# Pooled attention in a fused attention and two-MLP kernel: split float32r operands replaced by plain float32 on halves of the TensorE array

## The chip, the cores and the metric

One Trainium2 chip, one of its cores. The metric is the device time of the whole program in microseconds. The kernel before takes 675.1 us (median of three runs, 675.06 to 675.31). The engines are named as in the profile: PE is TensorE (PEld its weight loads), DVE is VectorE, ACT is ScalarE, POOL is GpSimd, SP is SyncE, whose queue issues most DMAs.

## The reference

All inputs are float32: q, k and v of 2 batches x 8 heads x 1152 positions x 64, then two MLPs on the 1152 x 512 result.

```python
q_pool = q.reshape(B, H, S // 2, 2, D).mean(axis=3)        # 576 rows a head
scores = scale * np.matmul(q_pool, k.transpose(0, 1, 3, 2)) # 576 x 1152
scores = scores - np.max(scores, axis=-1, keepdims=True)
attn = np.exp(scores)
attn = attn / (np.sum(attn, axis=-1, keepdims=True) + 1e-09)
x = np.matmul(attn, v)                                      # then heads side by side: 1152 x 512
h = x @ w_in
g = s * np.maximum(h, 0) ** 2 + b
y = g @ w_out                                               # w_in 512 x 2048
out = ((y @ w_a) * (y @ w_b)) @ w_out2                      # w_a, w_b 512 x 1536
```

## The kernel before, in words

The 16 heads are worked through as eight pairs, `n` = 0 to 7. In a pair the 2 x 576 pooled rows of q make nine blocks of 128 rows (`ORDER`): four of the first head, a middle one with 64 rows of each head, four of the second. Block `i` of pair `n` has the number `g = 9 * n + i`.

Products are made in float32r, each operand as a high part and a low part (what the high part misses). A key tile `kc` holds the high parts of k in 64 of 128 columns and the low parts in the others, so that turned (transposed by a product with the identity, `k_tr`) both stand below each other on the 128 rows of the array. A block of scores is the turned k against `qh`, then against `ql`, in three pieces of 384 columns: two into one tile of two banks (`s_mm01`), the third into a bank of its own (`s_mm2`). The middle block takes twice as many, with `qm_h` and `qm_l`.

Then, for each block: two maxima on DVE and their combination (`s_max01`, `s_max2`, `s_comb`); exp with a running sum on ACT in pieces of 384 and 768 columns (`s_exp2`, `s_exp01`); the sum and its reciprocal on DVE; the multiplication of `e` by it on POOL (`s_norm`, L491). Nine turns on PE (L515) put `e` into PSUM in groups of four, four and one, where the third group's bank also takes three riding turns of k or pooled q for the next pair. ACT copies the turned block out as its high part (`p_h`, L529), DVE subtracts that for the low part (`p_l`, L535). P by v (`pv_mm`, L551) runs over nine chunks of 128 keys, high and low, for each head in one segment of 256 and one of 320 rows; v stands beside its low part in the 128 columns of the stationary operand. Results are copied out by ACT (L563), moved between partition halves by DMA on SP's queue (`pv_add`, six a pair), added on POOL and split into `xa_h` and `xa_l` (`x_split`, L94 and L97), the first MLP's input. POOL also pools q (L338) and splits k and v (L94, L97).

There are three `e` buffers, two two-bank tiles for the main scores, and four banks (`banks`) that last scores, turns and P by v take in turn (`bank`, `bank_read`).

The order of all engines' work is written out by hand: `SCHED` is one period, in which each word is a step and a block or chunk, and each prime puts the step one pair later. `steps()` unrolls it over the eight pairs, a few steps are then moved by name (`put`), and each engine works off its own instructions strictly in that order. At the last pair the order also takes in the first products of the first MLP (`MM`, with `Fa`, `Fd`, `Fp` on ACT, DVE and POOL) and weight conversions (`CV`). The MLPs that follow (L681, L1005) aren't touched by the change.

Of the kernel before, what the change touches and what calls it, by code (L numbers as in the profile page):

```python
# [27 lines left out]
A.0 PP.8' X2.1 Lb.7' EVh.8' P2.4' R.0 Fp.0''''''''''''''' hc.8' M01.2 Tb.8' Lc.8' P2.5' S2.2 hb.8' Lb.8' P2.6' Ta.8'
X01.1 M2.2 A.1 ha.8' N.0 C.2 P2.7' R.1 P2.8' PVc.2' Tb.0 PVd.2' S01.3 hb.0 La.8' X2.2 Lb.0
CV.8''''''''''''''''''''''''''''''''''''''''''''''''''''''''''' N.1 S2.3 PP.1 M2.3 Ta.0 PP.0 X01.2 Tc.1 ha.0 M01.3  # L30
EVh.1 La.0 hc.1 Tc.0 EVh.0 C.3 KS.0, hc.0 MM.0' EVl.1 Lc.1 X2.3 S01.4 S2.4 A.2 Ta.1 Lc.0 X01.3 Tb.1 R.2 ha.1 P3.0'
M01.4 P3.1' M2.4 A.3 La.1 hb.1 Lb.1 CV.0, P3.2' S01.5 N.2 P3.3' Tb.2 R.3 C.4 hb.2 Ta.2 XS.0' P3.4' P3.5' ha.2 P3.6'
N.3 M01.5 X2.4 Lb.2 P3.7' P3.8' MM.1''''''''''''''''''''''''''''''''''''''''''''''' La.2 X01.4 CV.6' CV.7' CV.2 S2.5
PP.2 Tc.2 PVc.3' CV.1, Tb.3 EVh.2 M2.5 S01.6 P0.0 PVd.3' P0.1 hc.2 Lc.2 P0.2 S2.6 P0.3 C.5 hb.3 Lb.3 A.4 PP.3 X2.5
X01.5 Fd.0'''''' QP.0, Tc.3 Ta.3 M01.6 EVh.3 P0.4 R.4 M2.6 hc.3 P0.5 ha.3 VS.1 Fa.0'' CV.4 S01.7 A.5 N.4 C.6 Lc.3 S2.7
R.5 X01.6 P0.6 P0.7 P0.8 La.3 X2.6 Ta.4 M01.7 A.6 Tb.4 M2.7 PVc.0 R.6 ha.4 N.5 XS.1' CV.5 PVd.0 hb.4 Tc.4 C.7 PP.4
S01.8 La.4 X2.7 Ta.5 Lb.4 hc.4 Tc.5 PP.5
""".split()

@with_exitstack  # L40
def kernel(
# [212 lines left out]

# [4 lines left out]

# [911 lines left out]
```

## Time and profile before

| | us |
|---|---|
| median of three runs | 675.1 |
| the profiled execution | 675.21 |
| its span, first to last instruction | 673.4 |
| PE busy (98% of the span) | 662.3 |
| DVE busy (76%) | 512.4 |
| ACT busy (59%) | 394.9 |
| POOL busy (53%) | 354.1 |
| mean granted TensorE clock, share of full speed | 0.999 |

The busy times are sums over the whole span, and the span has two parts: the attention up to about 260 us, in which all four engines are in use, and the MLPs after it, which are mostly PE's. Shares of the whole say little about either; the rows below are from stretches of the attention.

### The profile page before, as it was taken

How to read it: one execution, taken by the hardware profiler on the slowest of the kernel's cores; microseconds unless marked ns; L12 is line 12 of the kernel's file. 1: busy time of each engine (PE TensorE's matmuls, PEld its weight loads, DVE VectorE, ACT ScalarE, POOL GpSimd, SP SyncE). 2: the span in 40 equal slices, each digit the busy share in tenths (PEclk: the TensorE clock that was granted, in tenths of full speed). 3: DMA queues.
4: the chain of work that ended last, by engine and by line, in shares of the span. 5: the costliest groups of instructions: out<-in, count | busy, mean ns of one | idle time of the engine just before them, and what ended most of it. 6: DMA issues, size and time to landing. Idle time of an engine off the chain costs nothing.

```text
span 673.4 us, 12031 instructions
## 1 busy us (share of the span) xinstructions
PE 662.3 (98%) x4446; PEld 635.8 (94%) x4446; DVE 512.4 (76%) x1007; ACT 394.9 (59%) x869; POOL 354.1 (53%) x316
## 2 busy tenths in 40 slices
PE   7999999999999999999999999999999999999997
PEld 6899999999999989999999999999999999988885
DVE  6999999999999995683554654888988787886431
ACT  6999999999999984464442242335343434434321
POOL 5779897978889693775454553400424542340000
PEclk9999999999999999999999999999999999999999
DMA  7122231413221023331322311420132323233004
GB/s 235 46 81 70 65 89 51 120 39 96 57 85 50 14 74 92 100 124 62 108 82 63 125 63 63 151 100 1 63 126 68 121 70 120 70 112 133 0 1 140
DMA packets 29275, 56.04 MB, mean 83 GB/s; under 512 B 2336, under 2 KB 6048, under 8 KB 29216
## 3 DMA queue, kind: packets, MB, share of 16 engines
q1 hardware_dynamic: 29136, 55.14, 26.0%
q8 instruction: 35, 0.57, 0.3%
q14 instruction: 24, 0.20, 0.1%
q10 hardware_dynamic: 80, 0.13, 0.1%
HBM read 49.81 MB, written 2.36 MB: 77 GB/s over the span
## 4 chain that ended last, share of the span: by engine, by line
PE 91%; DVE 3%; POOL 1%; DMA 1%; ACT 1%; issue 1%; SPq 0%; POOLq 0%; ACTq 0%; DVEq 0%
PE ps L681 29%; PE pp L681 17%; PE pv L551 11%; PE pp L1005 11%; PE s L423 8%; PE t L515 8%; PE s L430 4%; PE t L363 2%; PE t L383 1%; DMA xs<-tmp 1%; DMA qm<-in_q_dram 1%; DVE e L947 1%; DVE wl L165 0%; POOL e L491 0%; DVE f L143 0%
## 5 line engine op out<-in xcount | busy, mean ns | idle before, releaser
L491 POOL TENSOR_SCALAR e<-e,sm 128x1152 f32<-128x1152 f32 (+1 forms) x73 | 88.9, 1222 | 29.2 <-DVE sm L484 16.0
L1020 POOL TENSOR_TENSOR ab<-ab,at 128x576 f32<-128x576 f32 x24 | 35.0, 1478 | 91.1 <-ACT ab L1015 87.2
L515 PE MATMUL t<-identr,er 128*128 128x128 f32 x648 | 76.9, 245 | 2.9 <-POOL e L491 1.6
L515 PEld LDWEIGHTS t<-identr,er 128*128 128x128 f32 x648 | 65.4, 140 | 11.5 <-POOL e L491 2.4
L819 POOL TENSOR_SCALAR r<-r,sb_s,sb_b 128x384 f32<-128x384 f32 (+1 forms) x46 | 38.5, 848 | 61.0 <-DVE r L816 61.0
L535 DVE TENSOR_TENSOR p3l<-t,p3h 128x512 fp32r<-128x512 f32 (+1 forms) x120 | 64.6, 552 | 5.9 <-ACT p3h L529 4.3
L452 DVE TENSOR_REDUCE sm<-s 128x1 f32<-128x768 f32 x72 | 68.2, 947 | 0.1
L472 ACT ACTIVATE e<-s,sm 128x768 f32<-128x768 f32 x72 | 67.1, 932 | 0.5 <-DVE sm L460 0.4
L529 ACT CAST p3h<-t 128x512 fp32r<-128x512 f32 (+1 forms) x120 | 55.5, 506 | 10.3 <-PE t L515 9.5
L811 ACT ACTIVATE qpl<-ps 128x384 f32<-128x384 f32 (+1 forms) x46 | 21.7, 503 | 67.7 <-PE ps L681 62.7
L816 DVE SCALAR_TENSOR_TENSOR r<-ps,qpl 128x384 f32<-128x384 f32 (+1 forms) x46 | 25.1, 570 | 37.7 <-ACT qpl L811 37.6
L535 DVE TENSOR_TENSOR p2l<-t,p2h 128x512 fp32r<-128x512 f32 (+1 forms) x96 | 51.3, 549 | 1.6 <-ACT p2h L529 1.1
L141 ACT ACTIVATE f<-raw 128x1024 f32<-128x1024 f32 x34 | 38.6, 1135 | 17.7 <-issue 11.1
L529 ACT CAST p2h<-t 128x512 fp32r<-128x512 f32 (+1 forms) x96 | 46.7, 519 | 3.1 <-PE t L515 1.2
L681 PE MATMUL ps<-xa_h,wh 128*128 128x384 f32 (+1 forms) x200 | 45.2, 329 | 0.6 <-DVE r L816 0.6
L551 PE MATMUL pv<-p3h,v 128*128 128x320 f32 x144 | 45.7, 328 | 0.0
L464 ACT ACTIVATE e<-s,sm 128x384 f32<-128x384 f32 x72 | 43.7, 607 | 2.2 <-DVE sm L460 1.4
L681 PE MATMUL ps<-xa_l,wh 128*128 128x384 f32 (+1 forms) x200 | 45.0, 328 | 0.0
L681 PE MATMUL ps<-xa_h,wl 128*128 128x384 f32 (+1 forms) x200 | 45.0, 328 | 0.0
L165 POOL TENSOR_TENSOR wl<-f,wh 128x1024 fp32r<-128x1024 f32 x16 | 40.5, 2528 | 7.1 <-ACT wh L197 5.9
L681 PE MATMUL ps<-gh,wl 128*128 128x384 f32 x192 | 43.7, 336 | 0.0
L681 PE MATMUL ps<-gh,wh 128*128 128x384 f32 x192 | 43.7, 336 | 0.0
(142 smaller groups left out, 2036.6 us busy)
## 6 DMA issues: line engine op xcount, KB each, us to landing
raw<-in_moe_w_out_dram SPq DMA_DIRECT2D x14, 1024.0 KB, 4.9
raw<-in_moe_w_in_dram SPq DMA_DIRECT2D x8, 1024.0 KB, 5.5
raw<-in_moe_w_a_dram SPq DMA_DIRECT2D x6, 1024.0 KB, 5.0
raw<-in_moe_w_b_dram SPq DMA_DIRECT2D x6, 1024.0 KB, 5.0
vn<-in_v_dram SPq DMA_DIRECT2D x8, 576.0 KB, 3.9
...
```

The source lines that it names most:

```text
L165: eng.tensor_tensor(out=l, in0=f, in1=h.bitcast(F32), op=ALU.subtract)
L423: nc.tensor.matmul(ps[:, c, 0:384], w, x[:, c * 384:(c + 1) * 384], start=(z == 0), stop=(z == len(pr) - 1))
L452: nc.vector.reduce_max(small(g)[:, 0:1], SPS[g, 0][:, :, 0:384], axis=AX.XY)
L464: ins = nc.scalar.activation(out=e_tile(g)[:, 768:1152], in_=SPS.pop((g, 1))[:, 0:384], func=AF.Exp, bias=m[:, 2:3], accum_out=m[:, 3:4])
L472: ins = nc.scalar.activation(out=e_tile(g)[:, 0:768].rearrange("p (a c) -> p a c", a=2), in_=SPS.pop((g, 0))[:, :, 0:384], func=AF.Exp, bi ...
L491: E_DONE[g, c.start] = nc.gpsimd.tensor_scalar(out=e[:, c], in0=e[:, c], scalar1=m[:, 6:7], scalar2=1.0, op0=ALU.mult, op1=ALU.mult)
L515: t = nc.tensor.transpose(ps[:, i * 128:(i + 1) * 128].bitcast(F32R), er_at[g % 3][:, (c0 + i) * 128:(c0 + i + 1) * 128], identr)
L529: nc.scalar.copy(out=p_dst(g)[0][:, c0:c0 + n], in_=p_src(g, z))
L535: nc.vector.tensor_tensor(out=l, in0=p_src(g, z), in1=h.bitcast(F32), op=ALU.subtract)
L551: nc.tensor.matmul(ps[:, 0:N], V[n, hd][:, c].rearrange("p a d -> p (a d)"), p, start=(t == 0), stop=(t == 2 * NC - 1))
L681: nc.tensor.matmul(ps, a, c[:, o:o + n], start=(first and z == 0), stop=(last and z == 2), skip_group_check=more)
L1005: nc.tensor.matmul(ps, a[x], w2_at[kf][c], start=(kf == 0 and y == 0), stop=(kf == KF2 - 1 and y == 2))
```

## The change

The high and low parts of q, k, v and the turned blocks go. All products of the attention are plain float32.

- **Scores.** k is turned straight from the loaded tile, two chunks of 64 columns at a time, so even chunks stand on the array's upper 64 rows and odd ones on the lower (`X`, 640 columns). A main score is two 512-column products, one on each half of the rows, each into a bank of its own (`s_mm`); the ninth chunk's 128 columns follow on one half, upper or lower by the block's number (`s_mmx`). It stands in `X` twice; for that `load_k` loads it a second time. The middle block's products are split by output rows too, into quarters.
- **Turns.** `turn` makes two products, one for each half of 64 rows, with a 64-column identity, into two banks, one for each half (`ps_t`). Eight chunks of a block make a group (`p_tr`); ACT copies one bank out (`H`), DVE the other (`D`). The ninth chunks of two or three blocks come together with the turns of k or pooled q for the next pair in four further groups (`turns`, steps `U`, `UH`, `UD`).
- **P by v.** Two products of 288 columns for each chunk and head, one for each half of the array's columns, into the two partition halves of one bank (`pv_mm`). Four DMAs a pair put the results in place, with nothing to add.
- **Banks.** Four for main scores as before, two for the turns, two (`banks`) for last scores and P by v.
- **Buffers and loads.** Seven `e` buffers instead of three, two for k, and loads of k, v and q are issued up to three pairs ahead; the first loads of q go to ACT's queue.
- **Order.** A new `SCHED`, with no steps moved by name. `MM.0` of the first MLP is issued after all attention steps of the last pair.

The diff, cut to its core:

```diff
+D.5' X.7' T.6' M.0 MX.0 CV.5'' D.6' H.6' C.0 P0.3' A.7' P0.4' X.0 R.7' P0.5' U.2' UD.2' MM.0'''' S.1 UH.2' N.7' CV.2'
+P0.6' M.1 T.7' XX.0 H.7' SX.1 D.7' MX.1 S.2 C.1 T.8' A.0 R.0 XX.1 D.8' P0.7' H.8' P0.8' SX.2 X.1 M.2 MX.2 A.1 C.2 U.3'
+PVc.0' UH.3' XX.2 X.2 UD.3' S.3 M.3 SX.3 N.0 SX.4 MX.3 R.1 C.3 T.0 H.0 XX.3 S.4 D.0 M.4 MX.4 N.1 X.3 P1.0' P1.1' P1.2'
+CV.6'''' A.2 Fp.0''''''''''''''' A.3 CV.4' XS.0'' C.4 T.1
+CV.8''''''''''''''''''''''''''''''''''''''''''''''''''''''''''' R.2 R.3 D.1 S.5 XX.4 M.5 SX.5 MX.5 H.1 C.5 U.0 UD.0
+P1.3' X.4 N.3 P1.4' S.6 UH.0 N.2 X.5 T.2 S.8 XX.5 CV.1 SX.6 D.2 H.2 A.4 CV.7''''' M.6 T.3 P1.5' MX.6 P1.6' R.4 A.5 N.4
+C.6 CV.0, D.3 H.3 Fd.0''''''' P1.7' XX.6 QP.1, R.5 P1.8' X.6 M.8 PVd.0' SX.8 T.4 S.7 MX.8 PVc.1' SX.7 A.6 PVd.1' N.5
+H.4 C.8 XX.8 D.4 R.6 U.1 N.6 P0.0 M.7 X.8 QP.0,, UD.1 MM.1''''''''''''''''''''''''''''''''''''''''''''''' P0.1 A.8
+P0.2 MX.7 Fa.0'''' R.8 UH.1 T.5 C.7 S.0, XX.7 H.5 SX.0, N.8
...
     ps_s01 = s01.enter_context(tc.tile_pool(name="ps_s01", bufs=2, space=PSUM))
-    banks = [right(att, f"ps_{i}", 1, space=PSUM) for i in range(4)]
+    ps_t = [right(att, f"ps_t{i}", 1, space=PSUM) for i in range(2)]
+    banks = [right(att, f"ps_{i}", 1, space=PSUM) for i in range(2)]
+    NE = 7
+    ex_p = right(att, "ex", 1)
+    e_at += [ex_p.tile([128, S], F32, tag=f"e{i}", name=f"e{i}") for i in range(3, NE)]
+    pt = right(att, "pt", 1).tile([128, 2, NC, SP], F32, tag="pt", name="pt")
...
-    kc_p = right(att_in, "kc", 1)
+    k_p = right(att_in, "kn", 2)
+    free, held = list(range(2)), {}
...
+            KN[n] = k_p.tile([128, 2, NC + 1, D], F32, tag="kn", name="kn")
         o = slice(max(part - 1, 0), 2 if part != 1 else 1)
-        nc.sync.dma_start(out=KN[n][:, o], in_=k[b, h + o.start:h + o.stop].rearrange("h (p c) d -> p h c d", p=128))
+        src = k[b, h + o.start:h + o.stop].rearrange("h (p c) d -> p h c d", p=128)
+        nc.sync.dma_start(out=KN[n][:, o, 0:NC], in_=src)
+        nc.sync.dma_start(out=KN[n][:, o, NC], in_=src[:, :, NC - 1])
...
+    def q_step(n, hd):
+        q_pool(n, hd)
+            q_pool(n, 2)
+            load_q(n + 1)
+    def turn(ps, z, src):
+        for o, t in zip(HALF, ps):
+            nc.tensor.transpose(t[:, z * 64:z * 64 + 64], src(o), ident[o, o])
...
+        def mm(ps, w, r, c):
+            o = HALF[r]
+            if hd < 2:
+                nc.tensor.matmul(ps[:, 0:w], Q[n, hd][o, j * 128:(j + 1) * 128], X[n, hd][o, c], start=True, stop=True)
+            else:
+                for a in range(2):
+                    nc.tensor.matmul(ps[HALF[a], 0:w], Q[n, 2][o, a], X[n, a][o, c], start=True, stop=True, skip_group_check=True)
+    def s_mm(g):
+        SPS[g] = ps = ps_s01.tile([128, 2, 512], F32, tag="s01", name="s01")
+        for r in range(2):
+            s_parts(g)(ps[:, r], 512, r, slice(0, 512))
+    def s_mmx(g):
+        XPS[g] = ps = bank(("x", g), 2)
+        s_parts(g)(ps, 128, g % 2, slice(512, 640))
...
+        out = e_at[g % NE][:, 0:1024].rearrange("p (a c) -> p a c", a=2)
+        nc.scalar.activation(out=out, in_=SPS.pop(g), func=AF.Exp, bias=m[:, 2:3], accum_out=m[:, 4:5])
...
+        nc.scalar.activation(out=e_at[g % NE][:, 1024:S], in_=XPS.pop(g)[:, 0:128], func=AF.Exp, bias=m[:, 2:3], accum_out=m[:, 3:4])
+        bank_read(("x", g))
...
+        m, e = SM.pop(g), e_at[g % NE]
+        nc.gpsimd.tensor_scalar(out=e, in0=e, scalar1=m[:, 6:7], scalar2=1.0, op0=ALU.mult, op1=ALU.mult)
+    def t_tiles(key):
+        PS[key] = [p.tile([128, 512], F32, tag="t", name="t") for p in ps_t]
+        return PS[key]
+    def p_turn(ps, g, z, pos):
+        turn(ps, z, lambda o: e_at[g % NE][o, pos * 128:(pos + 1) * 128])
+    def p_tr(g):
+        ps = t_tiles(g)
+        for pos in range(8):
+            p_turn(ps, g, pos, pos)
+    def p_evac(g, k):
+        hd, j = ORDER[g % 9]
+        if hd < 2:
+            c = p_col(j) + 64 * k
+            out = pt[:, hd, 0:8, c:c + 64]
+        else:
+            out = pt[:, k, 0:8, 256:256 + NX]
+        copy(k, out, slots(PS[g], k, 0, 8))
+    TURN = [(0, 1), (2, 3, 4), (5, 6), (7, 8)]
+    def turns(n, u):
+        at = TURN[u] if n >= 0 else ()
+        if not at and n + 1 >= NP:
+            return
+        ps = t_tiles((n, u))
+        for z, i in enumerate(at):
+            p_turn(ps, 9 * n + i, z, 8)
+        if n + 1 < NP:
+            z, hd = len(at), u // 2
+            if u % 2:
+                src = qp_all.ap()
+                for j in range(4):
+                    turn(ps, z + j, lambda o: src[o, 4 * hd + j].rearrange("p a d -> p (a d)"))
+                if hd:
+                    turn(ps, z + 4, lambda o: src[o, 8].rearrange("p a d -> p (a d)"))
+                    Q[n + 1, 2] = q_p.tile([128, 2, 64], F32, tag="qt", name="qt")
+                Q[n + 1, hd] = q_p.tile([128, 512], F32, tag=f"q{hd}", name="q")
+            else:
+                for m in range(5):
+                    turn(ps, z + m, lambda o: KN[n + 1][o, hd, 2 * m:2 * m + 2].rearrange("p a d -> p (a d)"))
+                X[n + 1, hd] = x_p.tile([128, 640], F32, tag=f"x{hd}", name="x")
+                if hd:
+                    load_k(n + 3)
+    def turns_last(n, u, k):
+        if n < 0:
+            return
+        ps, hd = PS[n, u], u // 2
+        c = p_col(ORDER[TURN[u][0]][1])
+        copy(k, by_half(pt[:, hd, 8, c:c + 256], 2, k), slots(ps, k, 0, 2))
+        if u == 1:
+            copy(k, pt[:, k, 8, 256:256 + NX], ps[k][:, 128:192])
+    def turns_ride(n, u, k):
+        if n + 1 >= NP:
+            return
+        ps, z, hd = PS[n, u], len(TURN[u]) if n >= 0 else 0, u // 2
+        if u % 2:
+            copy(k, by_half(Q[n + 1, hd], 4, k), slots(ps, k, z, 4), qscale)
+            if hd:
+                copy(k, Q[n + 1, 2][:, k], ps[k][:, (z + 4) * 64:(z + 5) * 64], qscale)
+        else:
+            copy(k, by_half(X[n + 1, hd], 5, k), slots(ps, k, z, 5))
+    def pv_mm(n, hd, pos):
+        if pos == 0:
+            PV[n, hd] = bank(("pv", n, hd), 4 if (n, hd) == (NP - 1, 1) else 1)
+        ps = PV[n, hd]
+        for a in range(2):
+            nc.tensor.matmul(
+                ps[HALF[a], 0:HC], VN[n][:, hd, CHUNK[pos]], pt[:, hd, pos, a * HC:(a + 1) * HC],
+                start=(pos == 0), stop=(pos == NC - 1), skip_group_check=True,
             )
+        if hd and pos == NC - 1:
+            load_v(n + 2)
...
+        TMP[n, hd] = xs_p.tile([128, HC], F32, tag=f"t{hd}", name="tmp")
+        nc.scalar.copy(out=TMP[n, hd], in_=ps[:, 0:HC])
+        bank_read(("pv", n, hd))
+        if hd == 0:
+            XS[n] = xs_p.tile([128, SP], F32, tag="xs", name="xs")
+        for a in range(2):
+            nc.sync.dma_start(out=XS[n][HALF[hd], a * HC:(a + 1) * HC], in_=TMP[n, hd][HALF[a]])
+    def x_split(n, _):
+        o = slice(0, 128 if n < NP - 1 else 64)
+        split(*(t[o] for t in xa_at(n)), XS[n][o], nc.gpsimd, nc.gpsimd)
...
-        load_q(0, 1)
+        load_q(0, 1, nc.scalar)
-        load_q(0, 2)
+        load_q(0, 2, nc.scalar)
-        nc.vector.tensor_copy(out=identr, in_=ident)
-        for t in (qm_h, qm_l):
-            nc.vector.memset(t.bitcast(F32), 0.0)
-        warm = bank(("warm",), 1)
+        t_warm = t_tiles("warm")[0]
         for i in range(N_WARM):
-            nc.tensor.transpose(warm[:, 0:128], ident, ident)
-        bank_read(("warm",))
-        KC[0, 0] = kc_p.tile([128, NC, 2, D], F32R, tag="kc", name="kc")
-        thirds = [(KC[0, 0][:, c:c + 3], KN[0][:, 0, c:c + 3]) for c in range(0, NC, 3)]
-        for t, x in thirds:
-            nc.scalar.copy(out=t[:, :, 0], in_=x)
...
+            nc.tensor.transpose(t_warm[:, 0:128], ident, ident)
         q_pool(0, 0, nc.vector)
-        third_l(1)
-        third_l(2)
-        for t in "PP.2 PP.5 PP.3 PP.4 EVh.2 EVh.5 EVh.3 EVl.5".split():
+        early = "U.0 UH.0 UD.0 U.1 UH.1 UD.1".split()
+        for t in early:
             step(t, -1)
+        q_pool(0, 1)
+        q_pool(0, 2)
         load_q(1)
         load_k(1)
         unit_load()
-        order = list(steps())
-        order.remove(("XS.1", NP - 2))
-        order.insert(order.index(("N.6", NP - 1)) + 1, ("XS.1", NP - 2))
-        def put(t, n, behind):
-            if (t, n) in order:
-                order.remove((t, n))
-            order.insert(order.index(behind) + 1, (t, n))
-        put("EVh.4", -1, ("S01.0", 0))
-        put("PP.6", -1, ("S2.0", 0))
-        put("EVl.6", -1, ("C.1", 0))
-        put("X2.0", 0, ("X01.0", 0))
-        end = 1 + max(i for i, (t, n) in enumerate(order) if t.split(".")[0] in ("S01", "S2", "VS"))
+        load_v(1)
+        order = [(t, n) for t, n in steps() if n >= 0 or t not in early]
+        end = 1 + max(i for i, (t, n) in enumerate(order) if t.split(".")[0] in ("S", "SX"))
```

## Rows read from the trace of the kernel before

**Rows 1.** The page, part 4: the chain that ended last, by engine

```profile
PE 91%; DVE 3%; POOL 1%; DMA 1%; ACT 1%; issue 1%; SPq 0%; POOLq 0%; ACTq 0%; DVEq 0%
```

**Rows 2.** Busy by stage: length, PE, PEld, DVE, ACT, POOL, clock, DMA, GB/s

```profile
51.34:82.13 30.79, 30.75 (x244) 29.59 (x242) 29.35 (x80) 28.91 (x78) 26.27 (x26) 1.00 0.28 74
...
205.38:236.31 30.93, 30.91 (x241) 29.47 (x240) 30.55 (x81) 28.75 (x78) 24.62 (x25) 1.00 0.13 34
```

**Rows 3.** Timeline of PE, 110.1 to 128.3 us: start, length, instruction, count

```profile
110.14 0.80 PE L515 MATMUL t<-identr,er 128*128 128x128 f32 x8
110.78 0.38 PE L551 MATMUL pv<-p3h,v 128*128 128x320 f32 x1
...
119.60 0.51 PE L423 MATMUL s<-x,ql 128*128 128x384 f32 x2
119.95 0.33 PE L430 MATMUL s<-x,qh 128*128 128x384 f32 x1
...
120.41 0.28 PE L551 MATMUL pv<-p2l,v 128*128 128x256 f32 x1
120.53 0.28 PE L551 MATMUL pv<-p2h,v 128*128 128x256 f32 x1
...
128.10 0.31 PE L551 MATMUL pv<-p3h,v 128*128 128x320 f32 x1
128.25 0.30 PE L551 MATMUL pv<-p3l,v 128*128 128x320 f32 x1
```

**Rows 4.** Timeline of PE, warm-up: the second turn on, and the last two

```profile
1.62 1.06 PE L698 MATMUL warm<-ident 128*128 128x128 f32 x4
...
4.82 0.63 PE L698 MATMUL warm<-ident 128*128 128x128 f32 x2
```

**Rows 5.** Groups by form, stage 112.91 to 143.63: count, busy us, mean ns, idle before

```profile
L452 DVE TENSOR_REDUCE sm<-s 128x1 f32<-128x768 f32 x10 | 9.5, 948 | 0.0
L472 ACT ACTIVATE e<-s,sm 128x768 f32<-128x768 f32 x9 | 8.4, 935 | 0.0
...
L535 DVE TENSOR_TENSOR p3l<-t,p3h 128x512 fp32r<-128x512 f32 x10 | 6.7, 686 | 0.4 <-ACT p3h L529 0.2
L529 ACT CAST p3h<-t 128x512 fp32r<-128x512 f32 x10 | 5.9, 612 | 1.4 <-PE t L515 1.3
...
L464 ACT ACTIVATE e<-s,sm 128x384 f32<-128x384 f32 x9 | 5.5, 610 | 0.1
...
L455 DVE TENSOR_REDUCE sm<-s 128x1 f32<-128x384 f32 x9 | 5.0, 551 | 0.5 <-PE s L430 0.4
...
L97 POOL TENSOR_TENSOR kc<-kn,kc 128x576 fp32r<-128x576 f32 x2 | 2.9, 1430 | 0.2
...
L472 ACT ACTIVATION_READ_ACCUMULATOR e<-s,sm 128x1 f32 x9 | 2.1, 234 | 0.0
...
L480 DVE TENSOR_SCALAR sm<-sm 128x1 f32<-128x1 f32 x9 | 1.9, 208 | 0.0
L484 DVE RECIPROCAL sm<-sm 128x1 f32<-128x1 f32 x10 | 1.6, 156 | 0.0
...
L460 DVE TENSOR_REDUCE sm<-sm 128x1 f32<-128x2 f32 x10 | 1.5, 149 | 0.0
L529 ACT CAST p3h<-t 128x128 fp32r<-128x128 f32 x5 | 1.5, 297 | 0.0
...
L94 POOL TENSOR_SCALAR kc<-kn 128x576 fp32r<-128x576 f32 x2 | 1.4, 683 | 0.7 <-PE t L515 0.7
...
L400 ACT ACTIVATE qh<-t 128x384 fp32r<-128x384 f32 x2 | 1.1, 551 | 0.0
...
L563 ACT COPY tmp<-pv 128x320 f32<-128x320 f32 x2 | 0.9, 457 | 0.0
...
L400 ACT ACTIVATE qh<-t 128x128 fp32r<-128x128 f32 x2 | 0.6, 308 | 0.0
```

**Rows 6.** Line L1128: count, shortest, median and longest ns, first and last start

```profile
L1128 DVE COPY ab<-pp x4: 691/692/692, 657.5 to 661.5; 128x512 f32<-128x512 f32 x4
```

More of the change, by code (lines that the diff above doesn't have):

```diff
@@ L29 @@
[L29 to L33, printed above, removed]
@@ L296, in bank_read, with load_q @@
             free.append(held.pop(key)[0])
-    QN, QM, KN, VN = {}, {}, {}, {}
-    Q_READ, Q_DONE, E_READ = {}, {}, {}
-    SYNC = mybir.DependencyClass.Sync
-    def after(ins, earlier, why):
-        tc.add_manual_dep(ins.ins, earlier.ins.name, mybir.DependencyInfo(SYNC, why), reason="one room under two names")
-    KC, X, Q, V, E, RS, SPS = {}, {}, {}, {}, {}, {}, {}
+    QN, QM, KN, VN, X, Q, QT = {}, {}, {}, {}, {}, {}, {}
+    HALF = [slice(0, 64), slice(64, 128)]
     def bh(n):
         return n // HP, 2 * (n % HP)
-    def load_q(n, part=0):
+    def load_q(n, part=0, queue=nc.sync):
+        if n >= NP:
+            return
         b, h = bh(n)
@@ L504 @@
-    PTC = ((0, 4), (4, 4), (8, 1))
-    def t_bank(g, z):
-        if (g, z) not in TP:
-            TP[g, z] = bank(("t", g, z), 2 * (g >= 0) + (rides(g) if z == 2 else 0))
-        return TP[g, z]
-    def p_tr(g, z):
-        ps = t_bank(g, z)
-        c0, n = PTC[z]
-        for i in range(n):
-            t = nc.tensor.transpose(ps[:, i * 128:(i + 1) * 128].bitcast(F32R), er_at[g % 3][:, (c0 + i) * 128:(c0 + i + 1) * 128], identr)
-            if i == 0:
-                after(t, E_DONE[g, 512 if g == 0 and z else 0], mybir.DependencyReason.DATA)
-        E_READ.setdefault(g, []).append(t)
@@ L538 @@
-    TP = {}
-    PV = {}
-    XS = {}
-    def pv_mm(n, hd, big_seg, lo, hi):
-        key = (n, hd, big_seg)
-        N = 256 + NX if big_seg else 256
-        if lo == 0:
-            PV[key] = bank(("pv", key), 2 if n == NP - 1 else 1)
-        ps = PV[key]
-        for t in range(lo, hi):
-            c, x = divmod(t, 2)
-            p = p3[x][:, c, hd] if big_seg else p2[x][:, c]
-            nc.tensor.matmul(ps[:, 0:N], V[n, hd][:, c].rearrange("p a d -> p (a d)"), p, start=(t == 0), stop=(t == 2 * NC - 1))
@@ L608, in rides @@
-    def rides(g):
-        ahead, reads, _ = RIDES[g % 9]
-        return reads if g // 9 + ahead < NP else 0
-    def ride(n, i):
-        g = 9 * n + i
-        if rides(g):
-            pend[n, i] = RIDES[i][2](n + RIDES[i][0], t_bank(g, 2)[:, 128:512])
-    def evac(n, i, z):
-        if (n, i) in pend and pend[n, i][z]:
-            pend[n, i][z]()
-            bank_read(("t", 9 * n + i, 2))
-    def then_load(f, load):
-        def run(n, hd):
-            f(n, hd)
-            if hd == 1 and n + 1 < NP:
-                load(n + 1)
-        return run
+        m, e = SM.pop(g), e_at[g % NE]
@@ new lines, in xa_at, with pv_copy @@
+    def xa_at(n):
+        b, hp = divmod(n, HP)
+        return [x[:, hp, b * SP:(b + 1) * SP] for x in (xa_h, xa_l)]
+    def pv_copy(n, hd):
+        ps = PV[n, hd]
+        if (n, hd) == (NP - 1, 1):
+            h, _ = xa_at(n)
+            for a in range(2):
+                nc.scalar.copy(out=h[HALF[1], a * HC:(a + 1) * HC], in_=ps[HALF[a], 0:HC])
+                bank_read(("pv", n, hd))
+            return
+        TMP[n, hd] = xs_p.tile([128, HC], F32, tag=f"t{hd}", name="tmp")
+        nc.scalar.copy(out=TMP[n, hd], in_=ps[:, 0:HC])
+        bank_read(("pv", n, hd))
```

308 lines of the change are left out of this document (71 added, 237 removed).

## The prediction

> **What bounds the kernel now.** I read the chain that ended last first: 91% of the span is on PE [rows 1], so only time taken off PE, or a wait put in front of it, moves the end. Next I cut the attention into its repeating stages, one for each pair of heads, by the POOL instruction that writes xa_l. Six such stages follow one another from 51.34 to 236.31 us, 185.0 us together, 30.8 us each, at full granted clock [rows 2]. In each PE is busy for all but 0.04 us, DVE for 29.4, ACT for 28.9, POOL for 26.3 of the first, so PE sets the pace and DVE and ACT are only 5 to 6% behind it: a cheaper PE would soon meet them. The MLPs are untouched and PE-bound, so the sum is eight stages plus what happens at the two ends of the attention.
>
> What a PE instruction costs is the step from one start to the next, not its recorded length, which has a tail. The timeline gives 0.175 us for a 384-column score product (two in 119.60 to 119.95), 0.12 for a 256-column and 0.15 for a 320-column P by v product, 0.08 for a turn (eight from 110.14 to 110.78) [rows 3]. A stage has 60 score products (nine blocks with six, the middle one with twelve), 36 of each P by v kind and 108 turns (81 of e, 18 of k, 9 of q): 10.5 + 4.3 + 5.4 + 8.6 = 28.8 us. The 2.0 us that are left lie where the 15 groups of turns of the order meet products, 0.13 us a group; I use that as the price of a change of mode.
>
> **The change on PE.** Its products are plain float32, and the only plain float32 work in the trace is the 18 warm-up turns. Between the second, at 1.62, and the seventeenth, at 4.82, are fifteen steps, 0.213 us each [rows 4]. 128 columns at 2.4 GHz, the granted level, take 0.053 us: so plain float32 streams its columns four times, with nothing between, and the weight load hides behind it. Then, if the two halves of the array work at the same time:
> - Scores: 512 columns x 4 / 2.4 GHz = 0.853 us for a block's main part, 0.213 for its last 128 columns. Nine blocks: 9.6 us (10.5 now). The middle block runs as four quarters and costs the same.
> - P by v: 18 chunks of two 288-column products side by side, 0.48 each: 8.6 us (9.7 now).
> - Turns: 81 of e, 10 of k, 9 of q, each two 64-column products side by side, 0.107: 10.7 us (8.6 now). This part gets dearer. Its bounds: 0.107, if the loads of both halves are hidden as in the warm-up, and 0.16, if the two loads follow each other at the 0.08 of today's turns [rows 3]. I take 0.107, since the warm-up is the nearest row, float32 like the new turns.
> - Changes of mode: P by v splits the array by columns, all else by rows. The new order has 7 groups of P by v in a stage and 13 of turns. No row shows a change of the split. Nearest is the 0.13 us of a group of turns; bounds are 0, and 0.13 on all 20 groups. I take 7 x 0.13 = 0.9 us; the ends are 0 and 2.6.
>
> Sum: 9.6 + 8.6 + 10.7 + 0.9 = 29.8 us, against 30.8: 1.0 us a stage.
>
> **The other engines,** by rows of one stage [rows 5]. ACT: exp of 1024 columns, by the step from 384 to 768 (0.610 to 0.935), 1.15 us; of 128, 0.39; two reads of the sum, 0.46; one evacuation of 512, 0.61. That is 2.62 a block, 23.6 for nine. Riding turns (320 columns at 0.457, 256 at 0.43 between its rows for 128 and 384, last chunks at 0.297) 3.5, two P by v copies 0.85: 28.0 us, 1 less than now. DVE: maxima 1.21 and 0.29, three small ones 0.51, and the plain copy that replaces the subtraction: no gain, since a 512-column copy out of PSUM takes 0.691 [rows 6] where the subtraction took 0.686. Nine blocks 24.3, rides 3.4: 27.7 us, 1.6 less. POOL loses the k and v splits (1.43 + 0.68, four times: 8.4 us) and two adds, and falls from 26.3 to under 18. So the gain on PE isn't eaten by a total: 28.0 lies under 29.8, though a stage can't fall far below 29.3, where ACT would be as full as DVE is now (95%).
>
> **Hand-over of the turn banks.** Each half of the turns has one bank, so the next group waits until both copies of the last are done. In the new order the least PE work between two groups is a main score and a last score, 1.07 us. Against it: the tail of a float32 turn (the last warm-up turn ends 0.42 after its start, 0.21 past its step [rows 4]) plus a DVE copy of 0.69 [rows 6], 0.90, with 0.17 left for signals. Where an exp (1.15 and its 0.23 us read) stands ahead of the copy, PE waits instead. I cost it at 0; one such miss in a stage would be up to 1.2 us.
>
> **Ends and queues.** Before the first scores the splits of k fall away, and a second round of turns through one pair of banks comes in: 9 turns, two tails and two copies, some 2.4 us after the warm-up. At the finish, MM is issued after all of the last pair's attention and no longer fills it. SP issues per pair go from 11 to 10 (kn two for one, xs and tmp four for six), and what queues behind an xs move are loads for pairs one to three ahead; the first q loads go to the idle ACT queue. I take both ends as 0, since nothing there repeats, with bounds of 3 us either way, about that start-up chain.
>
> **Sum.** Eight stages x 1.0 = 8 us. The profiled execution took 675.2 us (span 673.4, and 1.8 outside it that I leave as they are), 0.1 over the median. 675.2 - 8 = 667 us. Its own bounds: no price for mode changes, but ACT's floor of 29.3, 8 x 1.5 = 12, and 3 at the ends: 660; mode changes at 1.5 in place of 0.9, 5, and 2 lost at an end: 674. That is the likeliest case's range.
>
> **Rivals.**
> 1. *Mode changes decide: slower.* Place: each border of turns, scores and P by v. If all 20 groups pay 0.13, a stage is 28.9 + 2.6 = 31.5 us, +0.7: 681. If each P by v group instead empties the array at both its ends, for the 0.21 us tail of [rows 4], it is 28.9 + 14 x 0.21 = 31.8: 683. With a hand-over miss a stage on top (1.2), 693. It decides from 1.9 us a stage on (30.8 - 28.9). For it speaks that today's borders do cost; against, that today's are between two kinds of product, and the new turns and scores are of one kind. The Trainium skill, "TensorEngine Tiling (Array Packing)", Key Properties, states that changing the tiling mode drains the engine; no run here shows the new modes, and it gives no time.
> 2. *The weight loads set the turns: slower.* If a turn costs 0.16, 100 take 16 us and a stage 9.6 + 8.6 + 16 + 0.9 = 35.1: +4.3, eight times 34 us, 710. It decides from 0.117 a turn. For it: 128 weight columns are loaded for only 64 streamed. Against: the warm-up's loads hide wholly. The Trainium skill, "TensorE: Matmul & The Clock Gate", LDWEIGHTS, has a load take its columns / 1.2 GHz; by that two in a row would be an estimated 0.213 us a turn, a stage of 40.5 and 753 us, while the 0.08 of a load and a turn together in [rows 3] is below the 0.107 that it gives for one load.
> 3. *The halves don't overlap: far slower.* Main scores 17.1 (the middle block's quarters 3.4), last scores 2.1, P by v 17.3, turns 21.3: 57.8 a stage, about 890 us. All products of the trace use the whole array, so no row shows it; that the warm-up's loads run beneath the streaming of other turns shows at least that PE works on two instructions at once, hence a small chance. The Trainium skill, "TensorE: Matmul & The Clock Gate", Part 3, says that products on different row groups run at the same time, 3.07 times as fast for four of them; no run here shows it, and it tells of no float32.
> 4. *Nothing to see.* Mode changes come to 1.7 to 2.1 us, or ACT and DVE, still over 90% full, keep a stage at 30.6 to 31.0: 674 to 677.
>
> **How the numbers follow.** Forecast 0.54; rival 1, 0.20; rival 2, 0.11; rival 3, 0.08; rival 4, 0.07, which is the case of no change, taken as within 0.2% (1.35 us), about what a measurement of this kernel can tell. So faster 0.54, same 0.07, slower 0.39. The range takes in a stage of PE's bare 28.9 with an end gained (675.2 - 15 - 3 = 657) and rival 1 with a hand-over miss and an end lost (693 + 3 = 696); left out are rivals 2 and 3, 0.19.
>
> **What would show it.** In the profile after: stages of 29 to 30.5 us between xa_l writes; main score products whose two halves start within a few ns and step 0.85 us a block; a group of eight turns in 0.86 us (1.3 means rival 2, 1.7 rival 3); P by v at 0.48 a chunk; gaps at the borders of P by v of about 0.06 us each; ACT near 28 and DVE near 27.7 us a stage, POOL near 16.5. The prediction is wrong if PE waits for evacuations in each stage, if the borders cost 0.2 each, or if turns step by more than 0.117.

## The result and the profile after

The kernel after takes 655.7 us (median of four runs, 653.54 to 657.73) against 675.1 for the kernel before in the same session (674.84 to 675.31): a ratio of 0.971, interval 0.968 to 0.974. The direction was forecast, the size was not: 19.4 us were gained where 8 were expected, and the time lies just below the range's low end of 657. The profiled execution, the fastest of the four, took 653.54 us; its span is 651.8 us, 21.6 less than before. From the start to the first 384-column product of the MLPs, 251.04 us pass in place of 272.74, 21.7 less: the MLPs gained nothing.

The chain that ended last, by engine, answers to [rows 1]:

```profile
PE 92%; DVE 4%; ACT 2%; POOL 1%; issue 1%; POOLq 0%; DVEq 0%; ACTq 0%
```

Cut at the same POOL instruction as before, the attention repeats every 27.8 us. The first stage of a run of five, with the columns of [rows 2]:

```profile
73.81:101.61 27.80, 27.78 (x336) 17.13 (x332) 23.90 (x66) 21.39 (x57) 15.88 (x14) 1.00 0.28 78
```

PE is again busy for all but 0.02 us of a stage, at the same granted clock, so a stage is still the sum of PE's steps. It is 3.05 us shorter (30.83 to 27.78, the means of six and of five stages); eight times that is 24.4, and 2.7 us of it were lost again at the ends. DVE and ACT, which stood 5 to 6% behind PE, are now 14 and 22% behind (means of the five), further off than before.

PE's timeline in the stage from 101.61 to 129.36, with the columns of [rows 3]:

```profile
101.83 0.71 PE L343 MATMUL t<-ident,e 64*128 64x64 f32 x16
102.38 1.08 PE L371 MATMUL s<-x,q 64*128 64x512 f32 x4
...
106.12 0.66 PE L343 MATMUL t<-ident,e 64*128 64x64 f32 x16
106.61 1.08 PE L371 MATMUL s<-x,q 64*128 64x512 f32 x4
107.53 0.21 PE L343 MATMUL t<-ident,e 64*128 64x64 f32 x1
...
108.33 2.16 PE L512 MATMUL b<-pt,vn 128*64 128x288 f32 x16
110.42 0.37 PE L371 MATMUL b<-x,q 64*128 64x128 f32 x1
...
119.77 0.71 PE L512 MATMUL b<-pt,vn 128*64 128x288 f32 x4
120.41 0.71 PE L343 MATMUL t<-ident,e 64*128 64x64 f32 x16
```

A plain float32 product appears as two MATMUL records (four for the two halves of a score), a turn as one (sixteen for eight turns). Read by starts, eight turns take 0.49 (106.12 to 106.61) to 0.55 us (101.83 to 102.38): 0.066 us a turn, where 0.107 was forecast. The main score after them takes 0.92 (106.61 to 107.53), forecast 0.853. Four chunks of P by v take 2.09 (108.33 to 110.42), one takes 0.64 (119.77 to 120.41): 0.48 for each further chunk, as forecast, and 0.16 on top of a group.

The largest groups by form in that stage, with the columns of [rows 5]:

```profile
L393 DVE TENSOR_REDUCE sm<-s 128x1 f32<-128x1024 f32 x9 | 11.0, 1220 | 1.3 <-PE s L371 0.8 <-POOL e L423 0.3 <-PE s L374 0.2
L512 PE MATMUL b<-pt,vn 128*64 128x288 f32 x76 | 10.9, 416 | 0.0
L406 ACT ACTIVATE e<-s,sm 128x1024 f32<-128x1024 f32 x9 | 10.1, 1118 | 1.4 <-POOL e L423 0.9 <-DVE sm L401 0.5
...
L343 PE MATMUL t<-ident,e 64*128 64x64 f32 x162 | 8.7, 228 | 0.0
```

The single prices of DVE and ACT came as forecast: the maximum over 1024 columns 1.22 (1.21 forecast), the exp 1.12 (1.15), DVE's copy 0.69 (0.69). The idle times of PE's groups are 0.0: no turn waits for an evacuation (the copy of a turn bank out of PSUM) here.

What the ends lost was lost at the start. PE's waits in the first 50 us (us in total, times, longest), of the kernel after and then of the kernel before:

```profile
PE s L371 <- ACT e L406: 2.5, 3, 1.5
PE t L343 <- POOL e L423: 2.4, 2, 1.6
```

```profile
PE t L515 <- POOL e L491: 1.4, 1, 1.4
```

All waits of the two lists, whose longest are shown, but for the wait of the warm-up for its identity (1.4 in both), come to 6.4 us after and 3.0 before. The first score starts at 7.99 us, where it started at 6.76; the larger part of the loss is waiting for the exp and the multiplication of the first blocks. Behind the last stage PE waits twice for ACT's copy of a turn bank, 0.82 and 0.67 us, 1.5 together; but before the change it waited 1.7 us in its finish (236.31 to 273 us), so nothing was lost there. 3.4 more at the start and 0.2 less at the finish are 3.2, near the 2.7.

### The profile page after: what moved, and what is told of

It reads as the page before. It is cut to its first block, busy times and chain, and to the rows that moved or that the text cites. A ratio compares the mean times of both kernels' runs of the same rounds, so it can differ in the third digit from the quotient of the medians.

```text
span 651.8 us, 13010 instructions
## 1 busy us (share of the span) xinstructions
PE 637.7 (98%) x5182; PEld 537.6 (82%) x5182; DVE 464.9 (71%) x892; ACT 332.5 (51%) x697; POOL 276.5 (42%) x228
## 4 chain that ended last, share of the span: by engine, by line
PE 92%; DVE 4%; ACT 2%; POOL 1%; issue 1%; POOLq 0%; DVEq 0%; ACTq 0%
PE ps L592 31%; PE pp L592 18%; PE pp L885 11%; PE b L512 11%; PE t L343 9%; PE s L371 8%; PE b L371 2%; PE s L374 1%; DVE sm L393 1%; ACT e L406 1%; PE t L606 1%; DVE e L827 1%; PE b L374 0%; POOL e L423 0%; DVE wl L160 0%
## 5 line engine op out<-in xcount | busy, mean ns | idle before, releaser
L423 POOL TENSOR_SCALAR e<-e,sm 128x1152 f32<-128x1152 f32 x72 | 87.8, 1225 | 89.2 <-DVE sm L401 57.4
L393 DVE TENSOR_REDUCE sm<-s 128x1 f32<-128x1024 f32 x72 | 87.9, 1220 | 10.8 <-PE s L371 6.6
L406 ACT ACTIVATE e<-s,sm 128x1024 f32<-128x1024 f32 x72 | 80.5, 1118 | 13.6 <-DVE sm L401 12.7
L343 PEld LDWEIGHTS t<-ident,e 64*128 64x128 f32 x1296 | 59.1, 138 | 29.3 <-issue 9.7
L512 PE MATMUL b<-pt,vn 128*64 128x288 f32 x576 | 81.8, 416 | 0.1
L371 PE MATMUL s<-x,q 64*128 64x512 f32 x256 | 72.8, 624 | 3.1 <-ACT e L406 2.5
L353 DVE COPY pt<-t 128x512 f32<-128x512 f32 (+1 forms) x112 | 59.7, 539 | 22.0 <-PE t L343 21.8
L343 PE MATMUL t<-ident,e 64*128 64x64 f32 x1296 | 69.4, 228 | 4.3 <-POOL e L423 2.4
L357 ACT COPY pt<-t 128x512 f32<-128x512 f32 (+1 forms) x112 | 51.5, 469 | 19.3 <-PE t L343 18.6
L693 ACT ACTIVATE qpl<-ps 128x384 f32<-128x384 f32 (+1 forms) x46 | 21.7, 503 | 69.4 <-PE ps L592 64.6
L592 PE MATMUL ps<-gl,wh 128*128 128x384 f32 x192 | 43.7, 336 | 0.0
```

Source lines behind the costliest of these rows:

```text
L343: nc.tensor.transpose(t[:, z * 64:z * 64 + 64], src(o), ident[o, o])
L353: nc.vector.tensor_copy(out=out, in_=in_)
L357: nc.scalar.copy(out=out, in_=in_)
L371: nc.tensor.matmul(ps[:, 0:w], Q[n, hd][o, j * 128:(j + 1) * 128], X[n, hd][o, c], start=True, stop=True)
L393: nc.vector.reduce_max(small(g)[:, 0:1], SPS[g], axis=AX.XY)
L406: nc.scalar.activation(out=out, in_=SPS.pop(g), func=AF.Exp, bias=m[:, 2:3], accum_out=m[:, 4:5])
```

## The experiments

The step to explain is the turn: 0.066 us for two products of 64 columns, where the prediction read four passes of its columns (0.107) out of the warm-up. Two readings were put up beside the prediction's own, with their numbers in the expectations. What parts them is whether the two halves of a turn run at the same time, so that one half alone would cost about as much as the pair, or whether a turn is cheap for a reason that has nothing to do with the halves; and with it, how many passes a turn takes, and at which clock level the warm-up row was. The second matter was the border between kinds of product, forecast at 0.13 for each group of P by v.

**e_bench: each kind of product by itself.** Behind the warm-up, runs of one kind each, on one half and on both halves in turn. Nothing reads their results; they make the kernel some 32 us longer (686.61 us, one run).

```diff
+        N_B = 24
+        for i in range(N_B):
+            nc.tensor.transpose(t0[:, i % 4 * 128:i % 4 * 128 + 128], ident, ident)
+        for i in range(N_B):
+            nc.tensor.transpose(t0[:, i % 8 * 64:i % 8 * 64 + 64], ident[HALF[0]], ident[HALF[0], HALF[0]])
+        for i in range(N_B):
+            nc.tensor.transpose((t0, t1)[i % 2][:, i // 2 % 8 * 64:i // 2 % 8 * 64 + 64], ident[HALF[i % 2]], ident[HALF[i % 2], HALF[i % 2]])
+        for i in range(N_B // 2):
+            nc.tensor.matmul(sc[:, 0], ident[HALF[0]], big_x[HALF[0], 0:512], start=True, stop=True)
+        for i in range(N_B // 2):
+            nc.tensor.matmul(sc[:, i % 2], ident[HALF[i % 2]], big_x[HALF[i % 2], 0:512], start=True, stop=True)
...
+        for i in range(N_B // 2):
+            nc.tensor.matmul(sc[:, 0, 0:128], ident, big_x[:, 0:128], start=True, stop=True)
```

> The changed kernel with eight runs of products put in behind the warm-up, 24 turns or 12 products each, whose results nobody reads; only their steps in the timeline count (the memset adds a wait, the whole some 35 us). Theory A (a plain float32 turn streams its 64 columns in fewer than four passes, by itself): turns on one half alone step by about 0.033 to 0.04 us, on alternating halves the same 0.033. Theory B (a turn costs 0.067 a half, and only the overlap of the halves makes it 0.033): alone 0.067, alternating 0.033. Theory C (four passes as in the prediction): alone 0.107, alternating 0.053 or more. Whole turns into four changing places of a bank: 0.213 if the warm-up's step is the turn's own cost, 0.107 or less if it came from writing the same 128 columns each time. Products of 512 columns: on one half alone 0.853 each, on alternating halves 0.427 each if the halves overlap fully, 0.853 if not at all. P by v's 288 columns: 0.48 on one half of the columns alone, 0.24 alternating. Whole-array products of 128 columns: 0.213.

PE's timeline of this kernel; L606 is the warm-up, L613 whole turns, L615 turns of one half, L617 of both in turn, L619 and L621 score products of one half and of both in turn, L623 P by v, L627 a whole product of 128 columns. Lines whose times lie inside another's are from narrower windows:

```profile
3.76 0.56 PE L606 MATMUL t<-ident 128*128 128x128 f32 x2
3.97 0.45 PE L606 MATMUL t<-ident 128*128 128x128 f32 x2
...
4.26 0.49 PE L606 MATMUL t<-ident 128*128 128x128 f32 x3
4.37 0.49 PE L606 MATMUL t<-ident 128*128 128x128 f32 x3
...
4.92 2.84 PE L613 MATMUL t<-ident 128*128 128x128 f32 x24
7.69 1.59 PE L615 MATMUL t<-ident 64*128 64x64 f32 x22
...
9.24 0.93 PE L617 MATMUL t<-ident 64*128 64x64 f32 x22
9.37 0.35 PE L617 MATMUL t<-ident 64*128 64x64 f32 x6
9.62 0.35 PE L617 MATMUL t<-ident 64*128 64x64 f32 x6
10.01 10.09 PE L619 MATMUL s<-e,ident 64*128 64x512 f32 x23
...
20.05 5.63 PE L621 MATMUL s<-e,ident 64*128 64x512 f32 x23
20.36 0.70 PE L621 MATMUL s<-e,ident 64*128 64x512 f32 x2
24.23 0.70 PE L621 MATMUL s<-e,ident 64*128 64x512 f32 x2
25.61 5.79 PE L623 MATMUL t<-e,ident 128*64 128x288 f32 x23
...
34.48 2.94 PE L627 MATMUL s<-e,ident 128*128 128x128 f32 x24
37.35 0.52 PE L343 MATMUL t<-ident,kn 64*128 64x64 f32 x10
```

- Whole turns step by 2.77 / 24 = 0.115 us. Two passes of 128 columns at 2.4 GHz are 0.107. The same turn in the warm-up steps by 0.21 (3.76 to 3.97) before about 4.1 us and by 0.11 (4.26 to 4.37) after it, with nothing changed in the program: the pace of PE doubled there. The trace's own records of the granted clock begin at 4.11 us in this run; in the kernel before they begin at 5.93, behind its last warm-up turn (5.04), and where there is no record the view shows 1.00. So 0.213 was two passes at 1.2 GHz, the lower level.
- A turn of one half steps by 0.062 (22 in 1.37), of both halves in turn by 0.035 (22 in 0.77): 0.07 for the pair, the change to the scores included, and 0.063 in the middle of the stretch (four pairs from 9.37 to 9.62). The halves run at the same time, two for one. A half turn loads as many weight columns as a whole one, 128, in little more than half the time; so the load isn't what sets the 0.115.
- A score product of 512 columns steps by about 0.86 alone (23 records in 9.93 us, 10.01 to 19.94, two to a product), which is four passes (0.853). In turn with the other half 23 records take 5.56 us with the change to P by v at the end; in the middle nine pairs of records, one of each half, take 3.87 (20.36 to 24.23), 0.43 a pair and 0.86 for both products. The halves overlap here too, two for one.
- A P by v product of 288 columns takes 0.49 on one half of the columns (23 records in 5.62 us, 25.61 to 31.23), and a pair of both halves as long, 0.485 (nine pairs of records in 2.18 us, in the middle of the next stretch).
- The whole product of 128 columns takes 2.87 / 12 = 0.239: four passes (0.213), where the whole turn of as many columns takes two.

So the reading with two passes and overlapping halves holds: a half alone costs 0.062 and the pair 0.063 to 0.07, not twice as much. The Trainium skill, "TensorE: Matmul & The Clock Gate", Part 1, says that TensorE works at 1.2 GHz at first and at 2.4 later; the doubling of the pace in the warm-up agrees with it.

**e_full_turns: the turns of e on the whole array.** One product of 128 columns in place of two of 64, in the main groups (eight of a block's nine turns), still into the two banks; the copies, left out here, put the results where they were.

```diff
-            p_turn(ps, g, pos, pos)
+            nc.tensor.transpose(ps[pos // 4][:, pos % 4 * 128:pos % 4 * 128 + 128], e_at[g % NE][:, pos * 128:(pos + 1) * 128], ident)
```

> The changed kernel with its main groups of turns on the whole array: eight 128x128 plain float32 turns in place of sixteen halves, chunks 0 to 3 in one bank and 4 to 7 in the other, copies of the same size. If the warm-up's 0.213 us is what a whole plain float32 turn costs, a group takes 1.70 us instead of 0.53 and a stage 9 x 1.17 = 10.5 us more: 27.8 to 38.3, the kernel about 740 us. If the warm-up's step came from its one place in PSUM, a group takes 0.53 to 0.85 and the kernel 656 to 679 us. The theory that the gain lies in overlap or fewer waits and not in the turns expects the second.

688.77 us (688.67 to 689.15), 1.020 of the kernel before, interval 1.019 to 1.022; 33 us over the kernel after. PE's timeline:

```profile
104.53 1.09 PE L435 MATMUL t<-ident,e 128*128 128x128 f32 x8
105.55 0.37 PE L371 MATMUL b<-x,q 64*128 64x128 f32 x1
```

Eight turns take 1.02 us, 0.128 each with the changes of split at both ends, between what the two theories gave. Against 0.066 that is 72 x 0.062 = 4.5 us a stage; the stages of this kernel are 32.60 us, 4.8 longer, and PE waits for nothing in them. The sign of the change hangs on this part: with everything else as in the kernel after, whole turns make it slower than before.

**e_half_by_half: the same half turns in another order,** eight of one half, then eight of the other.

```diff
-        for pos in range(8):
-            p_turn(ps, g, pos, pos)
+        for o, t in zip(HALF, ps):
+            for pos in range(8):
+                nc.tensor.transpose(t[:, pos * 64:pos * 64 + 64], e_at[g % NE][o, pos * 128:(pos + 1) * 128], ident[o, o])
```

> The changed kernel with the sixteen turns of a group in another order: all eight of the upper half, then all eight of the lower. Theory A (a half's turn is short by itself) expects a group still near 0.53 us and no change, 655 us within its noise. Theory B (0.067 alone, halved by overlap) expects 1.07 us a group, 9 x 0.53 = 4.8 a stage, about 693 us. Theory C (0.107 alone) expects 1.7 us a group and about 740 us.

666.35 us (666.15 to 667.77), ratio to before 0.988, interval 0.986 to 0.989: 10.7 us over the kernel after, with the same instructions. Its stages are 29.5 us, 1.7 longer, and PE waits for nothing in them. PE's timeline shows why it is not the full loss:

```profile
121.70 0.96 PE L436 MATMUL t<-ident,e 64*128 64x64 f32 x16
122.59 1.68 PE L513 MATMUL b<-pt,vn 128*64 128x288 f32 x12
...
126.33 0.96 PE L436 MATMUL t<-ident,e 64*128 64x64 f32 x15
127.07 0.69 PE L371 MATMUL s<-x,q 64*128 64x512 f32 x1
```

The result lies between the two expectations. Ahead of P by v, which splits the array by columns and so needs both halves, sixteen half turns take 0.89 us, close to the 0.96 of a sequence without overlap (16 x 0.06). Ahead of a score, that score's product for the half that is already free begins 0.74 us after the group, beneath the last turns of the other half. So the order in which instructions for the two halves are issued has a price of its own, and more than half of the gain (10.7 of 19.4 us) needs them alternating.

**e_more_groups: six further borders of P by v.** Six chunks are moved away from their groups, so that a stage has 13 groups of P by v in place of 7; no work is added. Shown are the stretches of `SCHED` that change.

```diff
-R.7' P0.5' U.2' UD.2'
+R.7' U.2' P0.5' UD.2'
...
-P1.0' P1.1' P1.2' CV.6'''' A.2 Fp.0''''''''''''''' A.3 CV.4' XS.0'' C.4 T.1
+P1.0' P1.1' CV.6'''' A.2 Fp.0''''''''''''''' A.3 CV.4' XS.0'' C.4 T.1 P1.2'
...
-X.4 N.3 P1.4' S.6 UH.0
+X.4 N.3 S.6 P1.4' UH.0
...
-P1.7' XX.6 QP.1, R.5 P1.8' X.6 M.8 PVd.0' SX.8 T.4 S.7
+XX.6 QP.1, R.5 X.6 M.8 PVd.0' SX.8 P1.7' T.4 P1.8' S.7
...
-P0.2 MX.7 Fa.0'''' R.8 UH.1 T.5 C.7
+MX.7 Fa.0'''' R.8 UH.1 T.5 P0.2 C.7
```

> The changed kernel with six chunks of P by v moved past one neighbouring score or group of turns each, so that a stage has 13 groups of P by v instead of 7 and nothing else changes. The trace after gives n chunks 0.48 n + 0.16 us. If the 0.16 is the price of a change between splitting by columns and by rows, a stage costs 6 x 0.16 = 1.0 us more and the kernel 8 us, 663. If the 0.16 is only the tail of whatever follows and hides elsewhere, no change. A moved chunk could also lengthen or shorten the cover of a hand-over by 0.48 us, up to 0.4 us a stage either way.

676.28 us (674.21 to 676.74), ratio to before 1.001, interval 1.000 to 1.002: the whole gain is gone. The stages are 30.88 us, 3.1 longer, 0.5 for each moved chunk. Not all of it is border. PE's waits between 80 and 200 us (total, times, longest), where the kernel after has none in its stages:

```profile
PE b L363 <- ACT e L402: 1.2, 4, 0.3
PE t L335 <- issue: 0.9, 4, 0.2
PE t L335 <- DVE sm L393: 0.6, 4, 0.2
```

2.7 us in four stages, 0.7 a stage; the other 2.4, 0.4 a moved chunk, are somewhat more than the 0.26 to 0.36 of two borders by the next experiment, and how they part between borders and scores that lost their overlap with neighbours isn't settled.

**e_bench2: the borders by themselves.** Behind the warm-up: P by v alone, then eight rounds each of a score and a P by v, a score and eight turns, eight turns and a P by v; and half turns in float32r, alone and alternating. Nothing reads their results (707.03 us, one run).

```diff
+        for i in range(24):
+            nc.tensor.transpose(t0[:, i % 8 * 64:i % 8 * 64 + 64].bitcast(F32R), identr[HALF[0]], identr[HALF[0], HALF[0]])
+        for i in range(48):
+            nc.tensor.transpose((t0, t1)[i % 2][:, i // 2 % 8 * 64:i // 2 % 8 * 64 + 64].bitcast(F32R), identr[HALF[i % 2]], identr[HALF[i % 2], HALF[i % 2]])
...
+        for i in range(8):
+            pv_pair()
+        for i in range(8):
+            score()
+            pv_pair()
+        for i in range(8):
+            score()
+            turn_8()
+        for i in range(8):
+            turn_8()
+            pv_pair()
```

> The changed kernel with more products behind the warm-up, results unread, for their steps alone. Float32r turns of 64 columns: if they stream once where plain ones stream twice, one half alone steps by about 0.04 us and the two halves together by 0.033 a pair or a little more (0.067 for a plain pair); if the load of 128 weight columns sets them, they step as the plain ones, 0.062 alone and 0.067 a pair. Borders: eight scores alone 0.93 each and eight chunks of P by v alone 0.53 each or less; taking turns, a score and a chunk together cost their sum plus two borders. If a border costs 0.13 us (half of the 0.26 that the trace after shows for a group of P by v: 0.16 inside it, 0.1 on its neighbours) that is about 1.7 us a round; with the 0.06 a border of the prediction about 1.55. Scores with groups of turns should show less than 0.06 a border, since both split the array by rows; turns with P by v 0.13.

PE's timeline:

```profile
20.17 4.10 PE L626 MATMUL t<-e,ident 128*64 128x288 f32 x32
24.20 1.13 PE L622 MATMUL s<-e,ident 64*128 64x512 f32 x4
...
25.90 0.70 PE L622 MATMUL s<-e,ident 64*128 64x512 f32 x2
...
39.22 1.08 PE L622 MATMUL s<-e,ident 64*128 64x512 f32 x4
...
40.63 1.08 PE L622 MATMUL s<-e,ident 64*128 64x512 f32 x4
...
49.67 0.71 PE L626 MATMUL t<-e,ident 128*64 128x288 f32 x4
...
50.96 0.71 PE L626 MATMUL t<-e,ident 128*64 128x288 f32 x4
```

P by v alone takes 4.03 / 8 = 0.50 a chunk with the change to the scores at the end, 0.485 without it (e_bench). A round with a score takes 1.70 (24.20 to 25.90). That is 0.28 more than 0.50 and the 0.92 of a score beside turns, and 0.35 more than 0.485 and the 0.86 of a score by itself: 0.14 to 0.18 for each of its two borders. A round of P by v with eight turns takes 1.29 (49.67 to 50.96), 0.26 to 0.30 more than its parts: 0.13 to 0.15 for each border. A round of a score and eight turns takes 1.41 (39.22 to 40.63), only 0.05 more than 0.86 and 0.50, what they take by themselves: hardly a border. So of these kinds the price lies where the array's split changes from rows to columns or back, 0.13 to 0.18 us each way. The Trainium skill, "TensorEngine Tiling (Array Packing)", Key Properties, says that a change of the tiling mode drains the engine; these rows agree, and 0.13 to 0.18 us is the price that it has here.

Half turns in float32r step by 0.080 alone (22 in 1.76 us) and 0.042 alternating (45 in 1.91): 0.084 a pair, dearer than plain float32's 0.063 to 0.07.

**e_fewer_groups and e_five_groups: fewer borders, in the hope of a better kernel.** One chunk of P by v is moved to its neighbours (six groups), then two more (five groups). Again the stretches of `SCHED` that change.

```diff
-P0.6' M.1 T.7' XX.0 H.7' SX.1 D.7' MX.1 S.2 C.1 T.8' A.0
+M.1 T.7' XX.0 H.7' SX.1 D.7' MX.1 S.2 C.1 T.8' P0.6' A.0
```

and for e_five_groups as well

```diff
-P1.3' X.4 N.3 P1.4' S.6
+X.4 N.3 S.6
...
-T.3 P1.5' MX.6 P1.6'
+T.3 P1.3' P1.4' P1.5' MX.6 P1.6'
```

> The changed kernel with one chunk of P by v moved next to two others, so that a stage has 6 groups instead of 7. If a group costs 0.26 us, 8 x 0.26 = 2 us less, about 653.5. If the moved chunk was needed as cover of a hand-over (a main score alone, 0.93, against tail and copies of about 0.95), no gain or up to 0.4 us a stage worse.

> The changed kernel with three chunks of P by v moved next to others, so that a stage has 5 groups instead of 7. If a group costs 0.26 us, 8 x 0.52 = 4 us less, about 651.5. If the moved chunks were needed as cover of two hand-overs, no gain or worse.

658.58 us (656.9 to 659.37), ratio to before 0.975, interval 0.973 to 0.977, and 664.45 (662.94 to 665.08), 0.984, interval 0.983 to 0.986. Neither beats the kernel after (0.971). The stages are 28.04 and 28.99 us. PE's waits from 80 to 200 us, of six groups and then of five:

```profile
PE t L335 <- POOL e L415: 1.1, 4, 0.3
```

```profile
...
PE t L335 <- DVE x L345: 0.8, 5, 0.2
```

Each saved group should give 0.26 us a stage. In six groups the moved chunk was the work that stood between a score and the turns of its multiplied `e`; without it the turns wait 0.3 us for POOL, and the stage is 0.26 longer, not shorter. With five, PE waits for three engines: for POOL as with six, 0.2 us a stage for ACT, and 0.2 for DVE's copy out of a turn bank. The zero that the prediction put on waits holds for the order as it is, and by little.

Part of what six groups lose is not the order's. The first score of the kernel after, and of the one with six groups:

```profile
7.99 1.13 PE L371 MATMUL s<-x,q 64*128 64x512 f32 x4 [0.61 <-DVE q L355]
```

```profile
8.23 2.08 PE L363 MATMUL s<-x,q 64*128 64x512 f32 x4 [0.61 <-DVE q L347]
```

It takes 0.94 us in one (to 8.93) and 1.84 in the other (to 10.07), PE's lower pace. The clock records begin at 6.24 us in the first and at 13.96 in the second, and the pace doubles there; from then on the second runs 2.0 us late (17.63 against 15.61 for the first product of the middle block). The profiled execution of e_more_groups starts in the same way. So the stages show what an order costs better than the whole time does.

That both halves of the turns might share a bank, which would free one for scores, wasn't tried.

## Why the prediction was right in direction and wrong in size

**The step that failed: the price of a turn.** "Plain float32 streams its columns four times" was read out of the warm-up row [rows 4], with the level taken as 2.4 GHz because the granted clock is shown as 1.00 there. It is two passes at 1.2 GHz (e_bench); the 1.00 stands there for want of a record. At the full level a turn on halves takes 0.066 us: 100 turns take 6.6 us a stage in place of 10.7, 4.1 less. "This part gets dearer" was the wrong sign: the 8.6 us of the turns before fall to 6.6. For scores and P by v the four passes were right, so one rule for all plain float32 work was the mistake; the only row was of a turn, and was used for both.

**Terms that were too small, and hid half of it.** Borders: the mechanism was named, and 0.13 us was near the right price (0.13 to 0.18), but it is paid at each of a group's two borders: 14 x 0.13 = 1.8, not 0.9. Main scores: 0.92 in place of 0.853. By itself a score takes 0.86, so the rest belongs to its place beside turns and borders, 9 x 0.07 = 0.6 more. P by v came as forecast. The middle block's quarters, which were to cost the same as other blocks, are a split of their own:

```profile
125.45 0.38 PE L371 MATMUL b<-x,q 64*128 64x128 f32 x2
125.82 0.44 PE L374 MATMUL b<-x,qt 64*64 64x128 f32 x4
126.19 0.71 PE L343 MATMUL t<-ident,e 64*128 64x64 f32 x16
126.92 1.09 PE L374 MATMUL s<-x,qt 64*64 64x512 f32 x8
127.97 1.68 PE L512 MATMUL b<-pt,vn 128*64 128x288 f32 x12
```

From 125.45 to 127.97 pass 2.52 us, where the paces by themselves would give 0.21 + 0.21 + 0.50 + 0.86 = 1.78. Of the 0.74 between, up to 0.18 is the border to P by v that is counted above; some 0.6 are left for three more changes of the split. With these, 29.8 - 4.1 + 0.9 + 0.6 + 0.6 = 27.8; measured are 27.78. The terms are read from neighbouring lines and overlap a little, so the close fit is partly luck, and the quarters weren't measured by themselves. Corrected for the turn alone, the sum would have been 25.7, as far off on the other side.

**The floor that wasn't one.** "A stage can't fall far below 29.3", ACT's full time, set the range's low end together with PE's bare 28.9. It adds up recorded lengths. The sum of the groups by form in the stage after is 26.3 us for ACT, but its busy time is 21.4 (27.7 and 23.8 for DVE; 38.7 and 28.9 for ACT before the change): instructions of one engine overlap in the records. ACT's 28.0 and DVE's 27.7 were lengths set against PE's steps. Read as busy time they leave 14 to 22% free, and no floor near PE.

**What held.** PE set the pace in each stage, as before. P by v's chunk, the exp, the maxima and the copies have the prices forecast, POOL fell to 15.9 us a stage (forecast under 18). The hand-over of the turn banks cost nothing in the stages, by the cover that was named; with five groups such a wait, for DVE's copy, comes to 0.2 us a stage, while the 0.3 of e_fewer_groups is a wait for POOL's `e`, which the prediction did not look at. The ends took 2.7 us, within the 3 stated, but only in part by the mechanisms named: the second round of turns at the start is 1.2, the rest of the start waits for ACT and POOL, and MM's absence cost the finish nothing (PE waits 1.5 us in it, 1.7 before).

**The rivals.** Rival 1, changes of mode, is real and at least twice as dear as I took it, but 1.8 us, or 2.4 with the quarters, can't outweigh the cheaper turns; e_more_groups, with its waits, shows the point from which it decides, 13 groups. Rival 2, loads that set the turns, is out: two loads and two products together take 0.07 us, so they are hidden, though e_full_turns shows that a turn at 0.128 would have made the change slower, near that rival's threshold of 0.117. By the Trainium skill, "TensorE: Matmul & The Clock Gate", LDWEIGHTS, one load of 128 columns takes an estimated 0.107 us (its columns / 1.2 GHz); a pair of turns that steps by 0.07 with two loads doesn't agree, and the measurement decides. Rival 3, halves that don't overlap, is out by e_bench for turns, scores and P by v. Rival 4, no change, is out by the ratio.
